# A windowed-attention and gated-product layer on one core: first chunk, load order, norms, transposes and last sums rearranged

## The chip, the core and the metric

The kernel runs on one core of a Trainium2 chip. The metric is the device time of one execution in microseconds (us), less is better. Three runs of the kernel before took 300.75 to 302.93 us, median 301.21.

## The reference, cut to what matters

```python
# x: 1 x 2048 x 512, wqkv: 512 x 1536, wo: 512 x 512, w_gate and w_up: 512 x 1792, w_down: 1792 x 512, all bf16
xn = (x - mean(x)) / sqrt(var(x) + 1e-5)              # over the 512 columns of a token
q, k, v = split_heads(xn @ wqkv)                      # 32 heads of 16
scores = q @ k.T * 16 ** -0.5                         # each token sees itself and the 255 before it
o = softmax(where(0 <= i - j < 256, scores, -1e9)) @ v
a = merge_heads(o) @ wo
b = ((xn @ w_gate) * (xn @ w_up)) @ w_down
out = x + a + b
```

## The kernel before

The 2048 tokens are 4 chunks (T = 0 to 3) of 4 blocks (b) of 128 tokens. Everything but the attention is a dense product of a chunk or a block. Attention goes by head group c (4 of 8 heads each), parity par (even or odd heads) and strip i (three strips of key blocks, `GROUPS`): 4 x 4 x 2 x 3 = 96 steps.

A step of `scores` runs four rows of the PE array side by side into S, one tile of four PSUM banks of which there is only one (`ps_s`); ScalarE takes exp of it into a P buffer (`ppool`, 5 buffers), and GpSimd zeroes what the window leaves out, with one `affine_select` for each masked block. Two steps later (LAG = 2), when all three strips of a head set are there, `values` multiplies them with V into `accb`; V has a column of ones, so that row 16 is the sum of the softmax. VectorE transposes `accb` (at), takes the reciprocal (rz), scales (on) and transposes again (OT).

The dense work is a list of fillers (`fillers`), each with a cost in units: one unit is a TensorE product of 512 columns. The order of the list is, for each T: down products and finish of the chunk before, 14 gate and up pairs of this chunk (`gu`), then V, K and Q of the next (`project`). Between the pairs of chunk T stand the norms of chunk T + 1: statistics, scale, apply and a transpose through TensorE of cost 1 (`norms`). `run` issues after each step so many fillers that the list is used up in proportion to the weight of the steps done, less a RESERVE of 28 units that is left over at the last step; a filler may have a step before which it must come and a `values` after which it may come. Of what is left, up to 22 units come ahead of the last `values`, the rest behind it, and at last the four `finish_late`.

TensorE, ScalarE, VectorE and GpSimd each run their instructions in the order in which they are written. The `ps_m` pool has 3 PSUM banks (tag M) for all dense sums: gp, up, psd, qkp, vp, xTp and last. `work` has 3 buffers of each tag, y among them.

The start (`setup`, then the loop in `run`): the four first blocks of x are loaded on the SP queue, Wqkv in three pieces (V columns, K, Q) on the ACT queue, then x 4 to 7, Wg and Wu by halves, x 8 to 15, Wd and Wo on SP. 36 products with an identity keep TensorE busy meanwhile (L85). Then each block b of chunk 0 is normalised (L114 to L133), transposed (L145, copied out by ScalarE at L148), multiplied for K and Q of head group 0 (`proj_qk_block`, L183) and for V (`proj_v`, L157), one block after the other. In later chunks VectorE copies the transposes out (L150).

The end: `finish_early` (L298 to L303) multiplies a block of the last chunk by three of the four parts of Wo, and VectorE adds x and keeps the sum in SBUF (y0); `finish_late` multiplies the last part into a fresh bank (last), VectorE adds y0 and the block is stored on SP.

Of the kernel before, what the change touches and what calls it, by code (L numbers as in the profile page):

```python
# [22 lines left out]
class Kernel:  # L23
    def __init__(self, ctx, tc, x, wqkv, wo, wg, wu, wd, out):
        self.tc, self.nc = tc, tc.nc
        _, S, D = x.shape
        self.S, self.D, self.F = S, D, wg.shape[1]
        assert D == 512 and S % 512 == 0 and self.F % 256 == 0
        self.NT, self.NCH, self.NF = S // 128, S // 512, self.F // 128
        self.x_d, self.out_d = x.flatten_outer_dims(), out.flatten_outer_dims()  # L30
        self.w_d = dict(qkv=wqkv, o=wo, g=wg, u=wu, d=wd)

        def pool(name, bufs, **kw):
            return ctx.enter_context(tc.tile_pool(name=name, bufs=bufs, **kw))

        self.const = pool("const", 1)
        self.chunk2 = pool("chunk2", 2)
        self.chunk3 = pool("chunk3", 3)
        self.ppool = pool("ppool", 5)
        self.work = pool("work", 3)  # L40
        self.xpool = pool("xpool", 4)
        self.small = pool("small", 4)
        self.ps_s = pool("ps_s", 1, space=bass.MemoryType.PSUM)
        self.ps_a = pool("ps_a", 1, space=bass.MemoryType.PSUM)
        self.ps_m = pool("ps_m", 3, space=bass.MemoryType.PSUM)


    def setup(self):
# [35 lines left out]
        for _ in range(36):  # L84
            nc.tensor.matmul(wps[:], lhsT=ident[:], rhs=ident[:], start=True, stop=True)  # L85
# [51 lines left out]
    def norm_transpose(self, t, on_act=False):  # L137
        nc = self.nc
        xn = self.xns.pop(t)
        T, b = divmod(t, 4)  # L140
        if b == 0:
            self.xnT[T] = self.chunk2.tile([128, 4, 512], BF16, tag="xnT", name=f"xnT{T}")
# [3 lines left out]
        dst = self.xnT[T][:, :, 128 * b:128 * b + 128]  # L146
        if on_act:
            nc.scalar.activation(out=dst, in_=ps[:], func=ACT.Copy)  # L148
        else:
            nc.vector.tensor_copy(out=dst, in_=ps[:])  # L150

    def proj_v(self, t):
        nc = self.nc
        T, b = divmod(t, 4)
        ps = self.ps_m.tile([128, 512], F32, tag="M", name="vp")
        for k in range(4):
            nc.tensor.matmul(ps[:], lhsT=self.xnT[T][:, k, 128 * b:128 * b + 128],  # L157
                             rhs=self.Wqkv[:, k, 1024:1536], start=(k == 0), stop=(k == 3))
# [3 lines left out]
    def proj_qk(self, T, c, is_k):  # L162
        nc = self.nc
        lo = 512 * is_k + 128 * c
        ps = self.ps_m.tile([128, 512], F32, tag="M", name="qkp")
        for k in range(4):
            nc.tensor.matmul(ps[:], lhsT=self.Wqkv[:, k, lo:lo + 128], rhs=self.xnT[T][:, k, :],  # L167
                             start=(k == 0), stop=(k == 3))
        if is_k:
            nc.vector.tensor_copy(out=self.K[T][:, c, :], in_=ps[:])  # L170
            nc.vector.tensor_scalar(out=self.Ko[T][:, c, :], in0=self.K[T][:, c, :],
                                    scalar1=self.odd[:, 0:1], scalar2=None, op0=ALU.mult)
        else:
            nc.vector.tensor_copy(out=self.Q[T][:, c, :], in_=ps[:])

    def proj_qk_block(self, b):

        nc = self.nc
        tok = slice(128 * b, 128 * b + 128)
        ps = self.ps_m.tile([128, 2, 128], F32, tag="M", name="qkb")  # L180
        for j, lo in enumerate((512, 0)):
            for k in range(4):
                nc.tensor.matmul(ps[:, j, :], lhsT=self.Wqkv[:, k, lo:lo + 128],  # L183
                                 rhs=self.xnT[0][:, k, tok], start=(k == 0), stop=(k == 3))
        nc.vector.tensor_copy(out=self.K[0][:, 0, tok], in_=ps[:, 0, :])
        nc.vector.tensor_copy(out=self.Q[0][:, 0, tok], in_=ps[:, 1, :])
# [68 lines left out]
    def gate(self, T, f):  # L255
        nc = self.nc
        if f == 0:
            self.hT[T] = self.const.tile([128, self.NF, 512], BF16, tag="hT", name=f"hT{T}")
        ps = self.ps_m.tile([128, 512], F32, tag="M", name="gp")
        for k in range(4):  # L260
            nc.tensor.matmul(ps[:], lhsT=self.Wg[:, k, 128 * f:128 * f + 128], rhs=self.xnT[T][:, k, :],  # L261
                             start=(k == 0), stop=(k == 3))
        self.gsb = self.work.tile([128, 512], BF16, tag="gsb", name="gsb")
        nc.vector.tensor_copy(out=self.gsb[:], in_=ps[:])  # L264

    def up(self, T, f):
        nc = self.nc
        ps = self.ps_m.tile([128, 512], F32, tag="M", name="up")
        for k in range(4):
            nc.tensor.matmul(ps[:], lhsT=self.Wu[:, k, 128 * f:128 * f + 128], rhs=self.xnT[T][:, k, :],  # L270
# [3 lines left out]
    def down(self, T, b, lo, hi):  # L274
        nc = self.nc
        if lo == 0:
            self.psd = self.ps_m.tile([128, 512], F32, tag="M", name="psd")
        for f in range(lo, hi):
            nc.tensor.matmul(self.psd[:], lhsT=self.hT[T][:, f, 128 * b:128 * b + 128],  # L279
                             rhs=self.Wd[:, f, :], start=(f == 0), stop=False)  # L280

    def wo(self, T, b, cs, ps, first):
        for c in cs:
            self.nc.tensor.matmul(ps[:], lhsT=self.OT[T][:, c, 128 * b:128 * b + 128],  # L284
                                  rhs=self.Wo[:, c, :], start=first and c == cs[0], stop=(c == cs[-1]))

    def store(self, T, b, ps, rest):
# [3 lines left out]
        nc.vector.tensor_tensor(out=y[:], in0=ps[:], in1=rest, op=ALU.add)  # L291
        nc.sync.dma_start(out=self.out_d[128 * t:128 * t + 128, :], in_=y[:])

    def finish(self, T, b):
        self.wo(T, b, (0, 1, 2, 3), self.psd, False)
        self.store(T, b, self.psd, self.x[:, 4 * T + b, :])

    def finish_early(self, T, b):  # L298

        nc = self.nc  # L300
        self.wo(T, b, (0, 1, 2), self.psd, False)
        self.y0[b] = self.const.tile([128, 512], F32, name=f"y0{b}")
        nc.vector.tensor_tensor(out=self.y0[b][:], in0=self.psd[:], in1=self.x[:, 4 * T + b, :], op=ALU.add)  # L303

    def finish_late(self, T, b):
        ps = self.ps_m.tile([128, 512], F32, tag="M", name="last")
        self.wo(T, b, (3,), ps, True)
        self.store(T, b, ps, self.y0[b][:])


    def fillers(self):
# [26 lines left out]
        def norms(T):  # L338
            t = 4 * T
            at = {f: [] for f in range(NF)}  # L340
            for b in range(4):
                at[b].append((0, lambda b=b: self.norm_stats(t + b)))
                at[6 + b].append((0, lambda b=b: self.norm_apply(t + b)))
                at[8 + b].append((1, lambda b=b: self.norm_transpose(t + b)))
            at[4].append((0, lambda: self.norm_scale(t)))
            return at
# [5 lines left out]
        for c in range(1, 4):  # L352
            qk(0, c, 6 * c)
        for T in range(NCH):
            if T:
                down(T - 1, 0)
                for b in range(4):
                    if b:
                        down(T - 1, b)
                    add(4, lambda T=T, b=b: self.finish(T - 1, b), None, NG * T - 1)  # L360
            gu(T, norms(T + 1) if T + 1 < NCH else {})
# [10 lines left out]
    def run(self):  # L372
        self.xns, self.stats, self.y0 = {}, {}, {}
        self.setup()
        NCH, NG, LAG = self.NCH, 24, 2
        RESERVE = 28
        self.new_chunk(0)
        self.norm_stats(0, 1)
        self.norm_scale(0, 1)
        for b in range(4):  # L380
            if b < 3:
                self.norm_stats(b + 1, 1)
                self.norm_scale(b + 1, 1)
            self.norm_apply(b)
            self.norm_transpose(b, True)
            self.proj_qk_block(b)
            self.proj_v(b)
        nc = self.nc
        nc.vector.tensor_scalar(out=self.Ko[0][:, 0, :], in0=self.K[0][:, 0, :],
                                scalar1=self.odd[:, 0:1], scalar2=None, op0=ALU.mult)  # L390
# [32 lines left out]
        fill(spent + 22, -1)  # L423
# [42 lines left out]
```

## Time and profile before

| | |
|---|---|
| runs of before | 300.75, 301.21, 302.93 us (median 301.21) |
| the profiled execution | 300.87 us, its span 299.1 us |
| TensorE matmuls busy | 274.7 us, 92% of the span |
| VectorE, ScalarE, GpSimd busy | 194.3, 181.5, 156.8 us |
| HBM read, written | 9.70 MB, 2.10 MB |

The span runs from the first to the last instruction of the execution; what lies around it is 1.8 us here. PE is TensorE, PEld its weight loads, DVE VectorE, ACT ScalarE, POOL GpSimd, SPq and ACTq the queues on which loads and stores are issued; "xTp<-ident,xn" reads "writes xTp from ident and xn", and L145 is line 145 of the kernel. Ends of matmuls are modelled, so a group of products is best read from one start to the next start.

### The profile page before, as it was taken

What the parts mean: (1) busy time and instruction counts of PE and PEld (TensorE: products, weight loads), DVE (VectorE), ACT (ScalarE), POOL (GpSimd) and SP (SyncE); (2) the same over time, 40 slices, a digit from 0 to 9 for tenths busy, and PEclk for the clock granted to TensorE, in tenths of its full rate; (3) what the DMA queues carried; (4) which work ended last, traced back from release to release, by engine and by line L of the source; (5) the groups of instructions that cost most, each with busy time, mean ns of one, the idle gap of its engine ahead of it and who ended that gap; (6) DMA issues with size and microseconds to landing.
All of it is one profiled execution on the core that took longest, in us unless ns stands there. A gap on an engine that the chain in (4) does not pass through costs nothing.

```text
span 299.1 us, 5877 instructions
## 1 busy us (share of the span) xinstructions
PE 274.7 (92%) x2424; PEld 119.6 (40%) x2460; DVE 194.3 (65%) x362; ACT 181.5 (61%) x118; POOL 156.8 (52%) x266
## 2 busy tenths in 40 slices
PE   6569989999999999999999999999999999999992
PEld 5333333433433444444344444443444443344440
DVE  3238898985823599984942489985763357877325
ACT  1247566568766756669566666758766675756610
POOL 3115565455565556656555466655556555555620
PEclk9999999999999999999999999999999999999998
DMA  7999000000000100000000000000000000000001
GB/s 234 370 369 324 3 3 0 3 0 2 1 20 18 37 0 2 1 2 2 0 19 19 20 18 3 0 2 1 2 0 20 35 20 1 2 0 2 2 0 70
DMA packets 10506, 12.17 MB, mean 41 GB/s; under 512 B 496, under 2 KB 10480, under 8 KB 10480
## 3 DMA queue, kind: packets, MB, share of 16 engines
q1 hardware_dynamic: 8896, 10.23, 10.1%
q10 hardware_dynamic: 1584, 1.57, 1.7%
q8 instruction: 19, 0.31, 0.4%
q14 instruction: 7, 0.06, 0.1%
HBM read 9.70 MB, written 2.10 MB: 39 GB/s over the span
## 4 chain that ended last, share of the span: by engine, by line
PE 68%; ACT 17%; DVE 6%; DMA 3%; issue 3%; POOL 1%; ACTq 1%; DVEq 0%
ACT P L209 16%; PE psd L279 15%; PE up L270 12%; PE gp L261 11%; PE S L201 10%; PE accb L234 7%; PE qkp L167 6%; DMA Wqkv<-in_A_wqkv_dram 3%; PE vp L157 2%; PE psd L284 2%; DVE at L245 1%; PE xTp L145 1%; DVE hT L272 1%; DVE st L114 1%; PE qkb L183 1%
## 5 line engine op out<-in xcount | busy, mean ns | idle before, releaser
L209 ACT ACTIVATE P<-S 128x2048 bf16<-128x2048 f32 (+2 forms) x96 | 170.0, 1771 | 86.8 <-PE S L201 79.1
L214 POOL TENSOR_SCALAR_AFFINE_SELECT P<-P 128x512 bf16<-128x512 bf16 x128 | 81.8, 639 | 75.2 <-ACT P L209 74.6
L218 POOL TENSOR_SCALAR_AFFINE_SELECT P<-P 128x512 bf16<-128x512 bf16 x112 | 72.8, 650 | 42.4 <-ACT P L209 42.4
L261 PE MATMUL gp<-xnT,Wg 128*128 128x512 bf16 x213 | 57.1, 380 | 1.4 <-DVE gsb L264 0.5
L270 PE MATMUL up<-xnT,Wu 128*128 128x512 bf16 x216 | 57.3, 380 | 0.5
L279 PE MATMUL psd<-Wd,hT 128*128 128x512 bf16 x213 | 51.7, 380 | 1.4 <-issue 1.3
L272 DVE TENSOR_TENSOR hT<-up,gsb 128x512 bf16<-128x512 f32 x56 | 38.5, 687 | 11.0 <-PE up L270 8.0
L245 DVE STREAM_TRANSPOSE at<-accb 128x512 f32<-128x512 f32 x32 | 22.9, 715 | 32.6 <-PE accb L234 32.2
L264 DVE CAST gsb<-gp 128x512 bf16<-128x512 f32 x56 | 38.1, 680 | 3.7 <-PE gp L261 3.4
L270 PEld LDWEIGHTS <-Wu 128*128 128x128 bf16 x224 | 19.9, 98 | 25.8 <-issue 5.4
L279 PEld LDWEIGHTS <-hT 128*128 128x128 bf16 x224 | 19.8, 97 | 25.9 <-issue 5.3
L261 PEld LDWEIGHTS <-Wg 128*128 128x128 bf16 x224 | 19.8, 98 | 25.0 <-issue 6.0
L167 PE MATMUL qkp<-xnT,Wqkv 128*128 128x512 bf16 x117 | 27.5, 380 | 0.5 <-issue 0.5
L234 PE MATMUL accb<-P,V 128*17 128x384 bf16 (+2 forms) x704 | 25.4, 276 | 0.0
L291 DVE TENSOR_TENSOR y<-psd,x 128x512 bf16<-128x512 f32 x12 | 8.3, 692 | 23.2 <-PE psd L284 23.2
L201 PE MATMUL S<-Q,Ko 32*128 32x256 bf16 (+2 forms) x352 | 18.4, 275 | 3.8 <-ACT P L209 3.6
L201 PE MATMUL S<-Q,K 16*128 16x256 bf16 (+2 forms) x352 | 18.4, 275 | 2.6 <-ACT P L209 2.4
L234 PEld LDWEIGHTS <-V 128*17 128x17 bf16 x704 | 13.8, 90 | 8.7 <-issue 5.5
L167 PEld LDWEIGHTS <-Wqkv 128*128 128x128 bf16 x120 | 10.7, 98 | 13.7 <-issue 2.5
L157 PE MATMUL vp<-Wqkv,xnT 128*128 128x512 bf16 x61 | 15.9, 392 | 0.3 <-issue 0.2
L201 PEld LDWEIGHTS <-Ko 32*128 32x128 bf16 x352 | 6.9, 92 | 22.6 <-issue 22.1
L201 PEld LDWEIGHTS <-K 16*128 16x128 bf16 x352 | 6.6, 92 | 22.6 <-issue 22.5
(44 smaller groups left out, 172.2 us busy)
## 6 DMA issues: line engine op xcount, KB each, us to landing
out_dram<-y SPq DMA_DIRECT2D x16, 128.0 KB, 1.7
Wg<-in_B_w_gate_dram SPq DMA_DIRECT2D x2, 896.0 KB, 9.9
Wu<-in_B_w_up_dram SPq DMA_DIRECT2D x2, 896.0 KB, 11.5
Wd<-in_B_w_down_dram SPq DMA_DIRECT2D x1, 1792.0 KB, 17.7
Wqkv<-in_A_wqkv_dram ACTq DMA_DIRECT2D x3, 512.0 KB, 6.0
x<-in_A_x_dram SPq DMA_DIRECT2D x1, 1024.0 KB, 14.6
x<-in_A_x_dram SPq DMA_DIRECT2D x4, 128.0 KB, 5.1
x<-in_A_x_dram SPq DMA_DIRECT2D x1, 512.0 KB, 8.2
```

The source lines that it names most:

```text
L167: nc.tensor.matmul(ps[:], lhsT=self.Wqkv[:, k, lo:lo + 128], rhs=self.xnT[T][:, k, :], start=(k == 0), stop=(k == 3))
L201: nc.tensor.matmul(S[:, e, col:col + n], lhsT=(self.Ko if par else self.K)[U][rows, c, 128 * j:128 * j + 128], rhs=self.Q[T][rows, c, 128 ...
L209: nc.scalar.activation(out=P[:, :, lo:hi], in_=S[:, :, lo:hi], func=ACT.Exp, scale=0.25)
L214: nc.gpsimd.affine_select(out=P[:, :, j:j + 128], in_=P[:, :, j:j + 128], pattern=[[0, 4], [1, 128]], compare_op=ALU.is_ge, fill=0.0, base ...
L218: nc.gpsimd.affine_select(out=P[:, :, j:j + 128], in_=P[:, :, j:j + 128], pattern=[[0, 4], [-1, 128]], compare_op=ALU.is_gt, fill=0.0, bas ...
L234: nc.tensor.matmul(acc[32 * e:32 * e + 17, 128 * q0:128 * q0 + n], lhsT=self.V[U][:, v, 8 * c + 2 * e + par, 0:17], rhs=P[:, e, col:col + ...
L245: nc.vector.transpose(out=at.rearrange("p b r -> p (b r)"), in_=acc[:])
L261: nc.tensor.matmul(ps[:], lhsT=self.Wg[:, k, 128 * f:128 * f + 128], rhs=self.xnT[T][:, k, :], start=(k == 0), stop=(k == 3))
L264: nc.vector.tensor_copy(out=self.gsb[:], in_=ps[:])
L270: nc.tensor.matmul(ps[:], lhsT=self.Wu[:, k, 128 * f:128 * f + 128], rhs=self.xnT[T][:, k, :], start=(k == 0), stop=(k == 3))
L272: nc.vector.tensor_tensor(out=self.hT[T][:, f, :], in0=ps[:], in1=self.gsb[:], op=ALU.mult)
L279: nc.tensor.matmul(self.psd[:], lhsT=self.hT[T][:, f, 128 * b:128 * b + 128], rhs=self.Wd[:, f, :], start=(f == 0), stop=False)
```

## The change

Five things are changed.

- Loads: everything goes on the SP queue in one order: x block 0, x block 1, x blocks 2 and 3, Wqkv's V, K and Q columns, the first halves of Wg and Wu, x 4 to 7, the second halves, Wd, Wo, x 8 to 15.
- First chunk (`first_chunk`): the norms run a block ahead of the transposes, the transposes a block ahead of V; K and Q of head group 0 are made for the whole chunk at once behind the four blocks, and K of head group 1 too. ScalarE copies Q out. There are 42 warm-up products in place of 36.
- Norms of later chunks: those of chunk 1 stand beside the gate and up products of chunk 0, with one block for every three pairs; those of chunks 2 and 3 stand beside the down products of the chunk before theirs. Each block has its own scale. The transpose is a DMA from the SP queue, of cost 0; `xnT` is laid out by block, then by part of the 512 columns.
- Last sums: the sums of the last chunk stay in PSUM, blocks 0 and 1 in banks of `ps_m`, blocks 2 and 3 in the four banks that S used. x is added to blocks 0 and 2 by a product with the identity, and to blocks 1 and 3 by VectorE on the way out; ScalarE copies blocks 0 and 2 out and stores them on the ACT queue.
- Sizes: 6 P buffers for 5, RESERVE 38 for 28, and up to 24 units for 22 ahead of the last `values`.

```diff
@@ pools and loads @@
-        self.ppool = pool("ppool", 5)
+        self.ppool = pool("ppool", 6)
...
-        for t in range(4):
-            nc.sync.dma_start(out=self.x[:, t, :], in_=xv[:, t, :])
+        for lo, hi in ((0, 1), (1, 2), (2, 4)):
+            nc.sync.dma_start(out=self.x[:, lo:hi, :], in_=xv[:, lo:hi, :])
         for lo in (1024, 512, 0):
-            nc.scalar.dma_start(out=self.Wqkv[:, :, lo:lo + 512], in_=wq[:, :, lo:lo + 512])
+            nc.sync.dma_start(out=self.Wqkv[:, :, lo:lo + 512], in_=wq[:, :, lo:lo + 512])
         h = self.F // 2
-        nc.sync.dma_start(out=self.x[:, 4:8, :], in_=xv[:, 4:8, :])
         for lo in (0, h):
             nc.sync.dma_start(out=self.Wg[:, :, lo:lo + h], in_=wg[:, :, lo:lo + h])
             nc.sync.dma_start(out=self.Wu[:, :, lo:lo + h], in_=wu[:, :, lo:lo + h])
-        nc.sync.dma_start(out=self.x[:, 8:NT, :], in_=xv[:, 8:NT, :])
+            if lo == 0:
+                nc.sync.dma_start(out=self.x[:, 4:8, :], in_=xv[:, 4:8, :])
...
+        nc.sync.dma_start(out=self.x[:, 8:NT, :], in_=xv[:, 8:NT, :])
...
-        for _ in range(36):
+        for _ in range(42):
@@ transposes @@
+            self.xnT[T] = self.chunk2.tile([128, 4, 4, 128], BF16, tag="xnT", name=f"xnT{T}")
+        if by_dma:
+            nc.sync.dma_start_transpose(out=self.xnT[T][:, b, :, :], in_=xn[:])
+            return
...
+        nc.scalar.activation(out=self.xnT[T][:, b, :, :], in_=ps[:], func=ACT.Copy)
...
-            nc.tensor.matmul(ps[:], lhsT=self.Wqkv[:, k, lo:lo + 128], rhs=self.xnT[T][:, k, :],
+            nc.tensor.matmul(ps[:], lhsT=self.Wqkv[:, k, lo:lo + 128], rhs=self.xnT[T][:, :, k, :],
@@ the first chunk (proj_qk_block and the loop in run go) @@
+    def first_chunk(self):
+        self.new_chunk(0)
+        for b in range(2):
+            self.norm_stats(b, 1)
+            self.norm_scale(b, 1)
+        for b in range(4):
+            self.norm_apply(b)
+            if b < 2:
+                self.norm_stats(b + 2, 1)
+                self.norm_scale(b + 2, 1)
+        self.norm_transpose(0, False)
+        for b in range(4):
+            if b < 3:
+                self.norm_transpose(b + 1, False)
+            self.proj_v(b)
+        self.proj_qk(0, 0, 1)
+        self.proj_qk(0, 0, 0, True)
+        self.proj_qk(0, 1, 1)
@@ down, store, finish @@
+            if T == self.NCH - 1 and b >= 2:
+                if b == 2:
+                    self.four = self.ps_s.tile([128, 4, 512], F32, tag="S", name="four")
+                self.psd = self.four[:, b, :]
+            else:
+                self.psd = self.ps_m.tile([128, 512], F32, tag="M", name="psd")[:]
...
+        if add:
+            nc.vector.tensor_tensor(out=y[:], in0=ps, in1=self.x[:, t, :], op=ALU.add)
+        else:
+            nc.scalar.activation(out=y[:], in_=ps, func=ACT.Copy)
+        (nc.sync if add else nc.scalar).dma_start(out=self.out_d[128 * t:128 * t + 128, :], in_=y[:])
...
     def finish_early(self, T, b):
-        self.wo(T, b, (0, 1, 2), self.psd, False)
-        self.y0[b] = self.const.tile([128, 512], F32, name=f"y0{b}")
-        nc.vector.tensor_tensor(out=self.y0[b][:], in0=self.psd[:], in1=self.x[:, 4 * T + b, :], op=ALU.add)
+        self.wo(T, b, (0, 1, 2), self.psd)
+        if b % 2 == 0:
+            self.nc.tensor.matmul(self.psd, lhsT=self.ident[:], rhs=self.x[:, 4 * T + b, :],
+                                  start=False, stop=False)
+        self.sums[b] = self.psd
 
     def finish_late(self, T, b):
-        ps = self.ps_m.tile([128, 512], F32, tag="M", name="last")
-        self.wo(T, b, (3,), ps, True)
-        self.store(T, b, ps, self.y0[b][:])
+        self.wo(T, b, (3,), self.sums[b])
+        self.store(T, b, self.sums[b], b % 2 == 1)
@@ fillers and run @@
+        def norms(T, at, step):
+            t, out = 4 * T, {}
             for b in range(4):
+                for k, f in enumerate((lambda b=b: self.norm_stats(t + b, 1),
+                                       lambda b=b: self.norm_scale(t + b, 1),
+                                       lambda b=b: self.norm_apply(t + b),
+                                       lambda b=b: self.norm_transpose(t + b, True))):
+                    out.setdefault(at + step * b + (0, 0, 1, 1)[k], []).append((0, f))
+            return out
...
-        for c in range(1, 4):
+        add(4, lambda: self.proj_qk(0, 1, 0), 6)
+        for c in range(2, 4):
             qk(0, c, 6 * c)
         for T in range(NCH):
             if T:
+                todo = norms(T + 1, 0, 1) if T + 1 < NCH else {}
                 for b in range(4):
+                    for g in todo.get(b, ()):
+                        add(*g)
+                    down(T - 1, b)
                     add(4, lambda T=T, b=b: self.finish(T - 1, b), None, NG * T - 1)
-            gu(T, norms(T + 1) if T + 1 < NCH else {})
+            for g in todo.get(4, ()) if T else ():
+                add(*g)
+            gu(T, norms(1, 1, 3) if T == 0 else {})
...
-        RESERVE = 28
+        RESERVE = 38
+        self.first_chunk()
...
-        fill(spent + 22, -1)
+        fill(spent + 24, -1)
```

## Rows read from the trace of the kernel before

**Rows 1.** Windows of 10 us: each engine's busy us (instructions), granted clock, DMA share, GB/s.
```profile
0.00:10.00 10.00, 5.21 (x44) 4.52 (x44) 2.88 (x9) 2.08 (x3) 2.79 (x13) 1.00 0.86 264
10.00:20.00 10.00, 6.43 (x43) 3.35 (x45) 3.95 (x13) 3.47 (x6) 1.71 (x4) 1.00 1.06 379
...
230.00:240.00 10.00, 9.84 (x91) 4.04 (x91) 3.52 (x7) 5.85 (x4) 6.00 (x10) 1.00 0.08 28
```

**Rows 2.** Waits of PE: us in total, times, longest us.
```profile
PE S L201 <- ACT P L209: 6.1, 23, 0.6
...
PE last L284 <- DVE OT L251: 0.7, 1, 0.7
PE gp L261 <- DVE gsb L264: 0.5, 1, 0.5
...
PE xTp L145 <- DVE xnT L150: 0.2, 1, 0.2
```

**Rows 3.** Timeline of the start: start us, us, engine, line, out<-in, count [idle before <-releaser].
```profile
1.42 4.02 PE L85 MATMUL wps<-ident 128*128 128x128 bf16 x36 [1.42 <-POOL ident L78]
...
3.31 0.69 DVE L114 BATCH_NORM_STATS2 st<-x 128x6 f32<-128x512 bf16 x1 [1.48 <-DMA x<-in_A_x_dram]
...
4.04 0.18 DVE L115 BATCH_NORM_AGGREGATE mv<-st 128x2 f32<-128x6 f32 x1
...
4.62 0.58 POOL L125 TENSOR_TENSOR rs<-ve,mhalf 128x1 f32<-128x1 f32 x1
...
6.40 0.38 DVE L133 TENSOR_SCALAR xn<-x,mv,rs 128x512 bf16<-128x512 bf16 x1
...
7.48 0.60 ACT L148 ACTIVATE xnT<-xTp 128x512 bf16<-128x512 bf16 x1 [3.57 <-PE xTp L145]
...
10.37 0.61 PE L183 MATMUL qkb<-xnT,Wqkv 128*128 128x128 bf16 x4 [1.65 <-DMA Wqkv<-in_A_wqkv_dram]
...
12.68 0.61 PE L145 MATMUL xTp<-ident,xn 128*128 128x128 bf16 x4
...
13.97 0.61 PE L183 MATMUL qkb<-xnT,Wqkv 128*128 128x128 bf16 x8 [0.69 <-ACT xnT L148]
...
14.41 1.03 PE L157 MATMUL vp<-Wqkv,xnT 128*128 128x512 bf16 x4
...
21.40 0.34 PE L201 MATMUL S<-Q,K 16*128 16x384 bf16 x4
...
28.23 1.04 PE L261 MATMUL gp<-xnT,Wg 128*128 128x512 bf16 x4
```

**Rows 4.** The chain that ended last: start us, us, what, matmuls.
```profile
66.86 0.61 PE vp L157 x2
...
109.93 0.86 PE up L270 x4
```

**Rows 5.** Timeline of TensorE beside chunk 1's gate and up products.
```profile
127.97 0.39 PE L145 MATMUL xTp<-ident,xn 128*128 128x128 bf16 x4
128.21 1.02 PE L261 MATMUL gp<-xnT,Wg 128*128 128x512 bf16 x4
```

**Rows 6.** Timeline of the end.
```profile
283.33 1.88 ACT L209 ACTIVATE P<-S 128x2048 bf16<-128x2048 f32 x1 [1.27 <-PE S L201]
...
289.71 0.83 PE L234 MATMUL accb<-P,V 128*17 128x128 bf16 x24
...
292.87 0.95 PE L284 MATMUL last<-Wo,OT 128*128 128x512 bf16 x3 [0.70 <-DVE OT L251]
293.31 1.87 DVE L291 TENSOR_TENSOR y<-last,y 128x512 bf16<-128x512 f32 x3
...
295.83 0.69 DVE L291 TENSOR_TENSOR y<-last,y 128x512 bf16<-128x512 f32 x1 [0.66 <-DMA out_dram<-y]
```

**Rows 7.** DMA issues: out<-in, queue, count, KB each, median us to landing.
```profile
out_dram<-y SPq DMA_DIRECT2D x16, 128.0 KB, 1.7
...
x<-in_A_x_dram SPq DMA_DIRECT2D x1, 1024.0 KB, 14.6
```

More of the change, by code (lines that the diff above doesn't have):

```diff
@@ L135, in norm_apply, with norm_transpose @@
         self.xns[t] = xn
-    def norm_transpose(self, t, on_act=False):
+    def norm_transpose(self, t, by_dma):
         nc = self.nc
@@ L141, in norm_transpose @@
         if b == 0:
-            self.xnT[T] = self.chunk2.tile([128, 4, 512], BF16, tag="xnT", name=f"xnT{T}")
+            self.xnT[T] = self.chunk2.tile([128, 4, 4, 128], BF16, tag="xnT", name=f"xnT{T}")
+        if by_dma:
+            nc.sync.dma_start_transpose(out=self.xnT[T][:, b, :, :], in_=xn[:])
+            return
         ps = self.ps_m.tile([128, 4, 128], BF16, tag="M", name="xTp")
@@ L145, in norm_transpose @@
             nc.tensor.transpose(ps[:, k, :], xn[:, 128 * k:128 * k + 128], self.ident[:])
[L146 to L150, printed above, removed]
+        nc.scalar.activation(out=self.xnT[T][:, b, :, :], in_=ps[:], func=ACT.Copy)
     def proj_v(self, t):
@@ L156, in proj_v @@
         for k in range(4):
-            nc.tensor.matmul(ps[:], lhsT=self.xnT[T][:, k, 128 * b:128 * b + 128],
+            nc.tensor.matmul(ps[:], lhsT=self.xnT[T][:, b, k, :],
                              rhs=self.Wqkv[:, k, 1024:1536], start=(k == 0), stop=(k == 3))
@@ L160, in proj_v, with proj_qk @@
                              func=ACT.Copy)
-    def proj_qk(self, T, c, is_k):
+    def proj_qk(self, T, c, is_k, on_act=False):
         nc = self.nc
@@ L172, in proj_qk @@
                                     scalar1=self.odd[:, 0:1], scalar2=None, op0=ALU.mult)
+        elif on_act:
+            nc.scalar.activation(out=self.Q[T][:, c, :], in_=ps[:], func=ACT.Copy)
         else:
             nc.vector.tensor_copy(out=self.Q[T][:, c, :], in_=ps[:])
[L176 to L186, printed above, removed]
+    def first_chunk(self):
[16 more added lines that the diff above has]
+        self.proj_qk(0, 1, 1)
     def parts(self, T, i):
@@ L260, in gate @@
         for k in range(4):
-            nc.tensor.matmul(ps[:], lhsT=self.Wg[:, k, 128 * f:128 * f + 128], rhs=self.xnT[T][:, k, :],
+            nc.tensor.matmul(ps[:], lhsT=self.Wg[:, k, 128 * f:128 * f + 128], rhs=self.xnT[T][:, :, k, :],
                              start=(k == 0), stop=(k == 3))
@@ L269, in up @@
         for k in range(4):
-            nc.tensor.matmul(ps[:], lhsT=self.Wu[:, k, 128 * f:128 * f + 128], rhs=self.xnT[T][:, k, :],
+            nc.tensor.matmul(ps[:], lhsT=self.Wu[:, k, 128 * f:128 * f + 128], rhs=self.xnT[T][:, :, k, :],
                              start=(k == 0), stop=(k == 3))
@@ L276, in down, with wo, store @@
         if lo == 0:
-            self.psd = self.ps_m.tile([128, 512], F32, tag="M", name="psd")
+            if T == self.NCH - 1 and b >= 2:
[4 more added lines that the diff above has]
+                self.psd = self.ps_m.tile([128, 512], F32, tag="M", name="psd")[:]
         for f in range(lo, hi):
-            nc.tensor.matmul(self.psd[:], lhsT=self.hT[T][:, f, 128 * b:128 * b + 128],
+            nc.tensor.matmul(self.psd, lhsT=self.hT[T][:, f, 128 * b:128 * b + 128],
                              rhs=self.Wd[:, f, :], start=(f == 0), stop=False)
-    def wo(self, T, b, cs, ps, first):
+    def wo(self, T, b, cs, ps):
         for c in cs:
-            self.nc.tensor.matmul(ps[:], lhsT=self.OT[T][:, c, 128 * b:128 * b + 128],
-                                  rhs=self.Wo[:, c, :], start=first and c == cs[0], stop=(c == cs[-1]))
-    def store(self, T, b, ps, rest):
+            self.nc.tensor.matmul(ps, lhsT=self.OT[T][:, c, 128 * b:128 * b + 128],
+                                  rhs=self.Wo[:, c, :], start=False, stop=(c == 3))
+    def store(self, T, b, ps, add):
         nc = self.nc
@@ L290, in store @@
         y = self.work.tile([128, 512], BF16, tag="y", name="y")
-        nc.vector.tensor_tensor(out=y[:], in0=ps[:], in1=rest, op=ALU.add)
-        nc.sync.dma_start(out=self.out_d[128 * t:128 * t + 128, :], in_=y[:])
+        if add:
[3 more added lines that the diff above has]
+        (nc.sync if add else nc.scalar).dma_start(out=self.out_d[128 * t:128 * t + 128, :], in_=y[:])
     def finish(self, T, b):
-        self.wo(T, b, (0, 1, 2, 3), self.psd, False)
-        self.store(T, b, self.psd, self.x[:, 4 * T + b, :])
+        self.wo(T, b, (0, 1, 2, 3), self.psd)
+        self.store(T, b, self.psd, True)
     def finish_early(self, T, b):
-        nc = self.nc
-        self.wo(T, b, (0, 1, 2), self.psd, False)
-        self.y0[b] = self.const.tile([128, 512], F32, name=f"y0{b}")
-        nc.vector.tensor_tensor(out=self.y0[b][:], in0=self.psd[:], in1=self.x[:, 4 * T + b, :], op=ALU.add)
+        self.wo(T, b, (0, 1, 2), self.psd)
[3 more added lines that the diff above has]
+        self.sums[b] = self.psd
     def finish_late(self, T, b):
-        ps = self.ps_m.tile([128, 512], F32, tag="M", name="last")
-        self.wo(T, b, (3,), ps, True)
-        self.store(T, b, ps, self.y0[b][:])
+        self.wo(T, b, (3,), self.sums[b])
+        self.store(T, b, self.sums[b], b % 2 == 1)
     def fillers(self):
@@ L336, in gu @@
                     add(*g)
-        def norms(T):
-            t = 4 * T
-            at = {f: [] for f in range(NF)}
+        def norms(T, at, step):
+            t, out = 4 * T, {}
             for b in range(4):
[L342 to L346, printed above, removed]
+                for k, f in enumerate((lambda b=b: self.norm_stats(t + b, 1),
[4 more added lines that the diff above has]
+            return out
         def down(T, b):
@@ L355, in fillers @@
             if T:
-                down(T - 1, 0)
+                todo = norms(T + 1, 0, 1) if T + 1 < NCH else {}
                 for b in range(4):
-                    if b:
-                        down(T - 1, b)
+                    for g in todo.get(b, ()):
+                        add(*g)
+                    down(T - 1, b)
                     add(4, lambda T=T, b=b: self.finish(T - 1, b), None, NG * T - 1)
-            gu(T, norms(T + 1) if T + 1 < NCH else {})
+            for g in todo.get(4, ()) if T else ():
+                add(*g)
+            gu(T, norms(1, 1, 3) if T == 0 else {})
             if T + 1 < NCH:
@@ L372, in run @@
     def run(self):
-        self.xns, self.stats, self.y0 = {}, {}, {}
+        self.xns, self.stats, self.sums = {}, {}, {}
         self.setup()
         NCH, NG, LAG = self.NCH, 24, 2
-        RESERVE = 28
[L377 to L390, printed above, removed]
+        RESERVE = 38
+        self.first_chunk()
         steps = [(T, c, par, i) for T in range(NCH) for c in range(4) for par in range(2) for i in range(3)]
```

## The prediction

> **What bounds the kernel now.** I read the windows first. In a window of the middle TensorE is busy 9.84 of 10 us, while VectorE, ScalarE and GpSimd have 3.5 to 6.0 us of work; in the first two windows TensorE is busy 5.21 and 6.43 us [rows 1]. So the middle is bound by TensorE's own work, and the start by something else. The waits of TensorE say how little can be won in the middle: it waits 6.1 us for the softmax engine in 23 short pieces, and under 1 us for anything else [rows 2]. The timeline of the start shows what holds it: the warm-up products end at 5.44, block 0's `xn` is made at 6.40, a K/Q product then waits until 10.37 for Wqkv, and the first scores begin at 21.40 [rows 3]. At the end the last values product starts at 289.71, TensorE waits 0.70 us for OT, and the fourth y waits 0.66 us for a store, because there are three y buffers [rows 6]. So 21.4 us lie before the first scores, 8.5 us behind the last values product, and about 269 us between, nearly all of it matmuls. A group of four 512-column products takes 0.86 us in the chain [rows 4], 0.216 us each; I call that one unit.
>
> **Start.** The loads' order changes, not their sum. 2.64 MB have moved by 10 us (264 GB/s over 10 us), and 379 GB/s is the rate of the next window [rows 1]. In the new order the V columns of Wqkv end at 1.05 MB, K at 1.57, Q at 2.10. If no stretch is faster than 379 GB/s, these pass by 10 - 1.59/0.379 = 5.8 us, 7.2 and 8.6 us; Wg's first half (3.0 MB) and Wu's (3.9 MB) by 11 and 13.4 us, x 4 to 7 by 14.8 us. None of these is late: V is needed at about 7.4 us, K at 12, the first gate product today at 28.23 [rows 3], so about 22 then. The wait until 10.37 goes.
>
> What is late next is the chain of norms. Block 0's statistics start about 3.2 us (3.31 today, with Wqkv sharing the engines); from there to the end of `rs` is 1.89 us (3.31 to 4.62 + 0.58), so `xn` 0 is ready at about 5.6. Each further block costs VectorE 0.69 + 0.18 + 0.38 = 1.25 us [rows 3]: 6.85, 8.1, 9.2. The warm-ups are 36 in 4.02 us, 0.112 us each, so 42 of them end at about 6.1 us: they, not the norm, release block 0's transposes. Those take 0.61 us (as at 12.68) and their copy 0.60 [rows 3]: `xnT` 0 stands at 7.35, while block 1 is transposed. V of block 0 then takes between 1.03 us (the row at 14.41) and twice that: a warm-up of 128 columns takes 0.112 us where a quarter of a unit is 0.054, a ratio of two, so the start runs at the lower of TensorE's two levels (1.2 GHz, though the granted clock reads 1.00), and the transposes at 12.68 still take the long time [rows 3]. I take 1.5: 8.9. Behind it come two blocks' transposes (0.25 to 0.4 each), and six groups of 0.86 us (three V, then K, Q and the K of group 1): 8.9 + 0.7 + 5.2 + 0.2 = 15.0 us to the first scores. ScalarE's eight copies (four xnT, four V at 0.60) and Q's fit beside this: Q's group ends about 14.2 and its copy at 14.9, under the K of group 1. Bounds: 14.3 if V 0 is already fast, 17.0 if the level rises no earlier than today (about 13 us), when three groups cost 0.86 more each. Gain at the start 21.4 - 15.0 = **6.4 us** (4.4 to 7.1).
>
> The K group of head group 1 is done there and leaves the paced work: **0.9 us** more.
>
> **Transposes of chunks 1 to 3.** Twelve TensorE transposes go. From one transpose's start to the next product is 0.24 us [rows 5], 0.25 with the switches: 12 x 0.25 = **3.0 us**. With them go twelve VectorE copies, and two waits of the first chunk, 0.2 for `xnT` and 0.5 for a `gsb` behind it [rows 2]: **0.7 us**. The norms of chunks 2 and 3 move beside the down products, where VectorE has 3.5 us of work in 10 [rows 1]. GpSimd gets twelve `rs` of 0.58 us (and their adds) instead of three larger ones, where it is busy 6.0 of 10 us; masks may come later by one of these, and the sixth P buffer and the two steps of lag cover that.
>
> The DMA transposes are in no row. Nearest rows: a 128 KB store lands in 1.7 us, a 1 MB load among other loads in 14.6 us [rows 7]; I take 5 us for a block, nearer the store in size. What hides it: in the first chunk the blocks are issued three gate/up pairs apart. Gate 0 starts at 28.23 and the next chunk's V at 66.86 [rows 3, 4], 2.76 us a pair, so 8.3 us apart, and the last block has two pairs and three V products, about 8.9 us. In later chunks the last transpose is a whole gate/up stage (28 groups, 24 us) ahead. Cost 0. On the SP queue the stores stand behind transposes that wait for `xn`; VectorE makes that promptly in this stage. A page of the Trainium skill speaks against this part: "VectorE: DVE Perf Modes", The three transpose paths, has a 128x128 transpose at 390 ns on TensorE and 1309 ns through the DMA, and its rules prefer TensorE where a PSUM destination will do. By it a block takes an estimated 4 x 1.3 = 5.2 us, which changes nothing in the sum as long as the time is hidden. No run here shows it yet.
>
> `xnT` is now laid out by block, so gate, up, K and Q products (28 x 4 x 4 + 8 x 4 x 4 = 576) read their moving operand in four runs of 128 columns. No row shows such a read. Below, nothing; above, I take four separate 128-column products: the eight at 13.97 take 0.61 us, 0.17 of it latency (1.03 less 0.86 for a group), so (0.61 - 0.17)/8 x 4 = 0.22 us a unit [rows 3], up to 6 ns over 0.216, so 3.4 us. I take 0, since the columns stay in one instruction.
>
> **Pacing.** The work list falls from 912 to 896 units and the reserve rises from 28 to 38, so a full step gets 9.5 units, not 9.8. More steps hold only two groups of four: 2 x 0.86 + 0.4 is less than an exp of 1.88 us and its start, and then the next scores wait for S, 0.27 us a time [rows 2]. About four more such waits: **+0.9 us**.
>
> **End.** Behind the last scores twelve units (2.6 us) are left before the third block's sums need S's banks, and the exp that must release them takes 1.88 us [rows 6]: no wait. Behind the last values product 12 units stand instead of 7, 2.6 us against a VectorE chain of 2.3 us (290.54 to 292.87), so the 0.70 us wait goes [rows 6]. Two identity products add 2 x 0.216 us. From the first late product to the end stays 6.2 us: ScalarE's copies spread the work, but the fourth y still needs the first one's buffer, so its store must land first, as at 295.83. Sum **-0.3 us**.
>
> **Sum.** -6.4 - 0.9 - 3.0 - 0.7 + 0.9 - 0.3 = -10.4 us. The profiled run took 300.87 us with a span of 299.1, within 0.1% of the median of 301.21; from the median this gives **290.8 us**.
>
> **Rivals.**
> A. The low level lasts: the first scores come at 17.0. Speaks for it: the transposes at 12.68 are slow today. Against: TensorE now works from 1.42 to 15 almost without a pause. 292.8 and up to 294.
> B. The other side: DMA transposes are slow and queue on SP. With D us a block, the fourth block of the first chunk lands 4D after the first's issue; it is needed 3 x 8.3 + 8.9 = 33.8 us after. From D = 8.5 TensorE waits 4D - 33.8 at the chunk's V. Past D = 11.8 us the wait is 13.4 us: slower than before by over 1% (304); at 11 the gain is gone (301). Later chunks have some 50 us for their four. For it: 14.6 us for 1 MB under load; against: 1.7 us for the same 128 KB.
> C. The four-run reads cost: 6 ns each give 294.2; 13 ns would take it within 1%.
> D. TensorE's freed time goes to the exp loop: each step without a values product (two thirds of some 80) waits 0.27 us, 14 us at most less today's 6.1, 4 to 7 us beyond my 0.9: 295 to 298.
>
> **Chances.** The forecast 0.64 (own range 288.5 to 293), A 0.10, C 0.09, D 0.07, B 0.10 (half of it within 1%, half slower). Within 1% (298.2 to 304.2) is about what no change looks like in this measurement. Faster 0.88 (forecast, A, most of C and D), same 0.07, slower 0.05. Range 287 to 296.5: below by the early start, no waits and a ppool that frees the exp (together 3.5 us); above it takes in A, C and the half of D.
>
> **What would show it.** The first scores near 15 us, with no wait for Wqkv; xnT transposes landing in about 5 us and no wait of V products on them; gate products still 0.86 us a group; S waits of TensorE near 7 us; no OT wait at the end, but still one wait for a store before the last y. A first-scores time above 17, a group above 0.88 us, or V products waiting for a DMA would each break a step.

## The result

The changed kernel takes 290.75 us (median of 4 runs, 290.48 to 292.21) against 301.39 for the kernel before (4 runs): ratio 0.965, 95% interval 0.960 to 0.970. The forecast was 290.8. Its profiled execution has a span of 289.2 us, 9.9 less than before's 299.1. (That execution took 292.21 us, 3.0 more than its span where the others have 1.7 to 1.8, so I go by spans inside a trace.) Some later runs of the kernel before have a lower mean granted clock (0.965 to 0.973) and take 302.5 to 305.2 us, so small differences are better read from spans than from a ratio.

The timeline of its start (columns as in [rows 3]):

```profile
1.42 4.66 PE L86 MATMUL wps<-ident 128*128 128x128 bf16 x42 [1.42 <-POOL ident L79]
...
5.88 1.27 PE L150 MATMUL xTp<-ident,xn 128*128 128x128 bf16 x8
...
7.20 1.07 PE L158 MATMUL vp<-Wqkv,xnT 128*128 128x512 bf16 x4
...
11.41 2.75 PE L168 MATMUL qkp<-xnT,Wqkv 128*128 128x512 bf16 x12
...
14.09 0.34 PE L212 MATMUL S<-Q,K 16*128 16x384 bf16 x4
```

The first scores start at 14.09, not 21.40, which is 7.3 us earlier, and no wait of TensorE for Wqkv is left. The waits of TensorE in the whole span (to set against [rows 2]):

```profile
PE S L212 <- ACT P L220: 7.7, 31, 0.7
PE four L300 <- ACT y L311: 1.5, 1, 1.5
...
PE up L281 <- DVE gsb L275: 0.5, 2, 0.3
```

The waits for S grew from 6.1 to 7.7 us, and a new wait of 1.5 us stands at the end. Beside the dense products TensorE waited 1.0 us for VectorE in the kernel before: 0.5 for gsb (VectorE's copy of a gate product) and 0.2 for xnT [rows 2], and 0.3 for hT (the gated product):

```profile
PE gp L261 <- DVE hT L272: 0.3, 1, 0.3
```

Now it waits 0.5 us, all of it for gsb. The end (columns as in [rows 6]):

```profile
279.52 0.83 PE L245 MATMUL accb<-P,V 128*17 128x128 bf16 x24
...
283.31 0.60 ACT L311 ACTIVATE y<-psd 128x512 bf16<-128x512 f32 x1 [9.36 <-PE psd L300]
...
285.17 0.38 PE L300 MATMUL four<-Wo,OT 128*128 128x512 bf16 x1 [1.47 <-ACT y L311]
285.82 0.69 DVE L309 TENSOR_TENSOR y<-four,x 128x512 bf16<-128x512 f32 x1 [1.61 <-DMA out_dram<-y]
```

And the DMA issues (as [rows 7], without a size): a transposed block lands 2.4 us after its issue (median of twelve).

```profile
xnT<-xn SPq DMA_TRANSPOSE x12, 2.4
```

From the first scores to the last values product the kernel before takes 289.71 - 21.40 = 268.3 us, the changed one 279.52 - 14.09 = 265.4: 2.9 us less. Behind the start of the last values product it takes 9.7 us where before took 9.4, but with 12 units there for 7 (1.1 us) and so 0.8 us less for the rest.

### The profile page after: what moved, and what is told of

Same layout as the page of the kernel before. It is cut to its first block, busy times and chain, and to the rows that moved or that the text cites. A ratio compares the mean times of both kernels' runs of the same rounds, so it can differ in the third digit from the quotient of the medians.

```text
span 289.2 us, 5817 instructions
## 1 busy us (share of the span) xinstructions
PE 274.1 (95%) x2396; PEld 116.8 (40%) x2396; DVE 185.1 (64%) x337; ACT 183.3 (63%) x121; POOL 161.7 (56%) x284
## 4 chain that ended last, share of the span: by engine, by line
PE 67%; ACT 22%; DVE 6%; issue 2%; POOL 1%; DMA 1%; ACTq 0%; DVEq 0%; POOLq 0%
ACT P L220 21%; PE psd L295 15%; PE S L212 10%; PE gp L272 9%; PE up L281 9%; PE accb L245 7%; PE qkp L168 5%; PE psd L300 3%; PE vp L158 3%; PE four L295 2%; PE wps L86 2%; DVE gsb L275 1%; DVE hT L283 1%; DVE at L256 1%; POOL P L225 1%
## 5 line engine op out<-in xcount | busy, mean ns | idle before, releaser
L272 PE MATMUL gp<-xnT,Wg 128*128 128x512 bf16 x224 | 57.8, 380 | 0.0
L295 PE MATMUL psd<-Wd,hT 128*128 128x512 bf16 x196 | 47.1, 380 | 0.0
L295 PEld LDWEIGHTS <-hT 128*128 128x128 bf16 x224 | 20.2, 98 | 25.9 <-issue 4.5
L168 PE MATMUL qkp<-xnT,Wqkv 128*128 128x512 bf16 x128 | 30.6, 380 | 0.0
L309 DVE TENSOR_TENSOR y<-psd,x 128x512 bf16<-128x512 f32 x13 | 9.0, 689 | 21.4 <-PE psd L300 21.4
L168 PEld LDWEIGHTS <-Wqkv 128*128 128x128 bf16 x128 | 11.3, 98 | 14.6 <-issue 2.9
L212 PEld LDWEIGHTS <-K 16*128 16x128 bf16 x352 | 7.4, 92 | 23.8 <-issue 23.3
L171 DVE CAST K<-qkp 128x512 bf16<-128x512 f32 x16 | 11.0, 687 | 8.5 <-PE qkp L168 8.4
```

The costliest lines, as they stand in the source:

```text
L212: nc.tensor.matmul(S[:, e, col:col + n], lhsT=(self.Ko if par else self.K)[U][rows, c, 128 * j:128 * j + 128], rhs=self.Q[T][rows, c, 128 ...
L295: nc.tensor.matmul(self.psd, lhsT=self.hT[T][:, f, 128 * b:128 * b + 128], rhs=self.Wd[:, f, :], start=(f == 0), stop=False)
```

## The experiments

**The start in two halves.** Three kernels put the new load order, the new first chunk with its 42 warm-ups, or both into the kernel before.

```diff
 loads:  the setup part of the change, nothing else
 chunk:  the kernel before with
+        self.first_chunk()                                # as in the change, xnT laid out as before
+        for _ in range(42):
...
+        add(4, lambda: self.proj_qk(0, 1, 0), 6)          # K of head group 1 leaves the list
 start:  loads and chunk
```

> The kernel before with the new load order alone. Theory that the start is bound by its chain of norms, copies and products: only the wait of the first K/Q product for Wqkv shortens, the first scores come about 2 us earlier (19.5), ratio 0.993. Rival, that the loads bind the start: first scores at 16 or before, ratio 0.98.

> The kernel before with the new first chunk and 42 warm-ups, loads as before (Wqkv on the ACT queue, beside x). Theory that the chain binds: first scores about 15.5 us, ratio 0.977. Rival, that the loads bind: the blocks of x and Wqkv arrive as late as before, first scores at 18 or later, ratio above 0.985.

> The kernel before with the new load order, the new first chunk and 42 warm-ups, all else as before. Theory that the parts add up: the first scores come at 14.1 us as in the changed kernel and the K group of head group 1 leaves the paced work, so the time falls by 7.3 + 0.9 = 8.2 us, ratio 0.973. Rival, that the earlier start is given back in waits for S or for weights in the first chunk: scores at 14.1, but the time falls by less than 5 us.

| kernel | first scores | span | median | ratio (95%) |
|---|---|---|---|---|
| before | 21.40 | 299.1 | 302.48 | |
| loads | 22.00 | 299.5 | 301.99 | 0.999 (0.994 to 1.004) |
| chunk | 17.54 | 296.3 | 298.51 | 0.986 (0.979 to 0.993) |
| start | 14.06 | 292.9 | 294.51 | 0.973 (0.964 to 0.981) |

(The median of before is that of 13 runs on the chip of these three kernels, 300.77 to 305.22 us; the ratios are to it. First scores and spans are those of the profiled executions.) The halves do not add up. With the load order alone the first scores come 0.6 us later, against both expectations; with the first chunk alone they come 3.9 us earlier, between the two expectations; with both, 7.3 us earlier. The timeline of TensorE in `loads` shows why the first is lost:

```profile
5.32 0.61 PE L146 MATMUL xTp<-ident,xn 128*128 128x128 bf16 x4
9.12 0.40 PE L184 MATMUL qkb<-xnT,Wqkv 128*128 128x128 bf16 x4 [3.19 <-DMA Wqkv<-in_A_wqkv_dram]
10.55 0.61 PE L184 MATMUL qkb<-xnT,Wqkv 128*128 128x128 bf16 x4 [1.03 <-DMA Wqkv<-in_A_wqkv_dram]
10.95 1.91 PE L158 MATMUL vp<-Wqkv,xnT 128*128 128x512 bf16 x4
```

Block 0's transposes start 1.5 us earlier (at 5.32; 6.84 in the kernel before), but the old first chunk wants K and Q first, which are now behind x and V in one queue. TensorE stands still from 6 to 9.1 us, and the two V products that follow take 1.91 and 1.83 us, not 1.03. Here the windows show the clock itself (granted clock before the DMA share):

```profile
6.00:8.00 2.00, 0.00 (x0) 0.00 (x0) 0.00 (x0) 0.56 (x1) 0.00 (x0) 1.00 0.98 310
8.00:10.00 2.00, 0.40 (x4) 0.23 (x4) 0.00 (x0) 0.00 (x0) 0.00 (x0) 0.94 1.07 357
10.00:12.00 2.00, 1.45 (x7) 0.86 (x8) 0.81 (x3) 0.00 (x0) 0.00 (x0) 0.50 1.05 397
```

After the idle stretch the granted clock is 0.50, the lower level (1.2 GHz). In `chunk` the late blocks of x do the same: TensorE waits 1.28 and 1.78 us for `xn`, and the clock of the windows from 8 to 12 us is 0.62 and 0.53:

```profile
6.94 0.40 PE L145 MATMUL xTp<-ident,xn 128*128 128x128 bf16 x4 [1.28 <-DVE xn L133]
9.12 0.61 PE L145 MATMUL xTp<-ident,xn 128*128 128x128 bf16 x4 [1.78 <-DVE xn L133]
9.52 1.91 PE L157 MATMUL vp<-Wqkv,xnT 128*128 128x512 bf16 x4
```

```profile
8.00:10.00 2.00, 0.88 (x6) 0.61 (x7) 1.93 (x6) 0.24 (x1) 0.89 (x3) 0.62 1.11 350
10.00:12.00 2.00, 2.00 (x10) 0.99 (x9) 0.65 (x2) 0.89 (x3) 0.89 (x2) 0.53 1.07 378
```

So x must come first and the products must ask for V first; either alone leaves TensorE waiting, and in these two traces the wait is paid a second time in the clock. A page of the Trainium skill says the same of the cause: "TensorE: Matmul & The Clock Gate", HAM oscillation, has the clock fall after a stretch in which TensorE idles; these windows agree (0.94, then 0.50). Not every wait is paid twice: in a trace below (`p5`) TensorE waits 0.58 us at the same place and stays fast.

`start` also answers its rival in part. It gains 7.3 us at the first scores and 0.9 for the K group, but the span falls by 6.2 only: its waits for S rise from 6.1 to 7.8 us, 1.7 us given back. So neither the theory (8.2 us) nor the rival (less than 5) came. The totals do not decide it: `start` is 8.0 us below the median of before on its chip and 6.9 below the 301.39 us of the result, and the ratio's interval is too wide to tell 6 from 8.

**The warm-ups (`w36`).**

```diff
-        for _ in range(42):
+        for _ in range(36):
```

> The changed kernel with 36 warm-up products for 42. Theory that the warm-ups only delay block 0: its transposes start at about 5.4 us for 5.88, the norms of blocks 1 to 3 then bind, and the first scores come 0 to 0.5 us earlier. Rival, that six more warm-ups bring TensorE to its upper level sooner: the first V product takes 1.9 us for 1.07 and the first scores come 1 to 3 us later.

290.47 us (290.43 to 290.81), first scores at 13.65, 0.44 earlier. Block 0's transposes start at 5.36 and are slow (0.61 us), those of block 1 take 0.40 and V 1.03. So, set against this execution, the six more warm-ups bought nothing and cost the 0.4 us that they take; in the total that is too small to tell from the changed kernel's 290.75. But the rival is not dead: the kernel `best` below also has 36, and in its profiled execution block 1's transposes are still slow:

```profile
6.43 0.61 PE L151 MATMUL xTp<-ident,xn 128*128 128x128 bf16 x4 [0.51 <-DVE xn L135]
```

Its first V product then takes 1.86 us, and the first scores come at 15.87, as the rival has it. In every trace here that has the new loads, the new first chunk and 42 warm-ups, the first V product takes 1.02 to 1.07 us. Whether six more warm-ups guard the start is open.

**TensorE transposes at the new places (`pet` and `pet2`).** In the changed kernel the later chunks' transposes go through TensorE again (four products of cost 1, VectorE copies them out); once right behind each norm, as the DMA is in the list, and once two places further on.

```diff
-            nc.sync.dma_start_transpose(out=self.xnT[T][:, b, :, :], in_=xn[:])
-            return
+            ...   # four nc.tensor.transpose into xTp, then
+            nc.vector.tensor_copy(out=self.xnT[T][:, b, :, :], in_=ps[:])
...
-                    out.setdefault(at + step * b + (0, 0, 1, 1)[k], []).append((0, f))
+                    out.setdefault(at + step * b + (0, 0, 1, 1)[k], []).append((int(k == 3), f))   # pet
+                    out.setdefault(at + step * b + (0, 0, 1, 3)[k], []).append((int(k == 3), f))   # pet2
...
-            for g in todo.get(4, ()) if T else ():             # pet2, and chunk 1's norms one place earlier
-                add(*g)
-            gu(T, norms(1, 1, 3) if T == 0 else {})
+            gu(T, norms(1, 0, 3) if T == 0 else {f - 4: todo[f] for f in todo if f >= 4})
```

> The changed kernel with the later chunks' transposes on TensorE, copied out by VectorE as in the kernel before, at their new places and with cost 1 in the list. Theory that a TensorE transpose costs its own time: twelve of 0.25 us, 3.0 us slower than the changed kernel, some 293.7 us. Rival, that the freed time goes to the waits for S: 1 us slower or less.

> The changed kernel with the later chunks' transposes on TensorE, two places of the list (two gate and up pairs, or two blocks of down products) behind their norms. Theory that a transpose on TensorE costs its own time where the norm is done by then, and that the 22 us of the run with transposes right behind their norms are waits of TensorE for xn: 3 us slower than the changed kernel, some 293.7 us. Rival, that a TensorE transpose costs more than its time at the new places (PSUM banks, copies): 8 us slower or more.

`pet` takes 312.19 us (310.50 to 314.90), ratio 1.035 (1.025 to 1.045): slower than the kernel before. Neither expectation held. The waits of TensorE say why, and the timeline what the longest of them brings:

```profile
PE xTp L147 <- DVE xn L134: 17.2, 13, 2.5
PE S L212 <- ACT P L220: 5.9, 24, 0.7
```

```profile
29.42 0.45 PE L147 MATMUL xTp<-ident,xn 128*128 128x128 bf16 x4 [2.50 <-DVE xn L134]
29.66 1.91 PE L272 MATMUL gp<-xnT,Wg 128*128 128x512 bf16 x4
```

Thirteen waits for `xn`, up to 2.5 us, twelve of them at the later chunks' transposes: TensorE runs in order, and a transpose written right behind its norm waits for VectorE, GpSimd's `rs` and VectorE again. On SP only stores stand behind the same wait. Behind the longest wait a gate group takes 1.91 us, not 1.03, and the granted clock of the window from 31 to 33 us is 0.50. 17.2 and twelve times 0.25 make 20.2 of the 21.4 us; the waits for S are 1.8 us fewer than in the changed kernel, and slow stretches such as this one weigh against that.

`pet2`, with the norm two places ahead as in the kernel before, takes 294.06 (293.57 to 295.77): 3.3 us more than the changed kernel, where 3.0 was expected, and no long wait for `xn`. The agreement is partly chance. Its waits of TensorE differ from the changed kernel's in two lines above all:

```profile
PE S L212 <- ACT P L220: 6.1, 25, 0.7
PE gp L272 <- DVE gsb L275: 2.1, 1, 2.1
```

Twelve transposes of 0.25 us are 3.0; the wait for gsb and one of 0.3 for xnT, for 0.5 in the changed kernel, add 1.9; the waits for S are 1.6 us fewer. So, by these rows, about half of the 3.0 us that the DMA transposes free comes back as waits for S, and the waits for VectorE that fall away bring the gain back to 3 us. Besides, the DMA lets norm and transpose be written at one place.

**Doubled DMA transposes (`dup`).**

```diff
...   # scratch: a tile of its own for each chunk
+            nc.sync.dma_start_transpose(out=self.scratch[:, b, :, :], in_=xn[:])
             nc.sync.dma_start_transpose(out=self.xnT[T][:, b, :, :], in_=xn[:])
```

> The changed kernel with every DMA transpose issued twice, first into a scratch tile. Theory that the DMA transposes lie wholly beside other work: within 0.5 us of the changed kernel although SP and the DMA engines carry twice the transposes. Rival, that they hold something up (the V products, or stores and y buffers behind them on SP): 1.5 us slower or more.

290.81 us (290.71 to 290.95): twice the transposes cost nothing that can be measured. They are hidden.

**The place of the norms, the P buffers, the end (`place`, `p5`, `oldtail`).** Three parts of the changed kernel undone one at a time.

```diff
 place:
-                todo = norms(T + 1, 0, 1) if T + 1 < NCH else {}
+                todo = {}
-            gu(T, norms(1, 1, 3) if T == 0 else {})
+            gu(T, norms(T + 1, 1, 3) if T + 1 < NCH else {})
 p5:
-        self.ppool = pool("ppool", 6)
+        self.ppool = pool("ppool", 5)
 oldtail:
-        RESERVE = 38
+        RESERVE = 28
...   # fill(spent + 22); finish_early and finish_late with y0 and a fresh bank, as before
```

> The changed kernel with the norms of chunks 2 and 3 beside the gate and up products (one block for every three pairs, as for chunk 1) in place of beside the down products; transposes by DMA. Theory that VectorE's load beside the gate and up products does not bind TensorE: within 0.5 us of the changed kernel. Rival, that the new place is what pays: 2 us slower or more, with TensorE waiting for gsb and hT.

> The changed kernel with 5 P buffers for 6. Theory that TensorE binds and the sixth buffer only frees ScalarE (its waits for GpSimd return from 2.8 to about 8 us): 0 to 0.7 us slower. Rival, that the sixth buffer pays: 2 us slower or more.

> The changed kernel with the end of the kernel before: sums of the last chunk added to x by VectorE and kept in SBUF, a last product into a fresh bank, a reserve of 28 units and 22 of them ahead of the last values product. Theory: the end brings next to nothing, 0 to 0.7 us slower, because the wait for OT (0.7 us) returns and two identity products (0.43 us) go. Rival, that keeping the sums in PSUM pays: 2 us slower.

`place` takes 292.20 us (291.81 to 292.79), 1.45 more: between the two expectations. TensorE then waits 1.7 us for `gsb` beside the gate and up products, where the changed kernel waits 0.5; that is 1.2 of it. Both kernels have a scale for each block, so this compares two places for the new norms; in the kernel before, with one scale for four blocks beside the gate and up products, the wait for gsb was 0.5 us.

```profile
PE up L281 <- DVE gsb L275: 1.7, 3, 1.1
```

`p5` takes 291.13 (290.95 to 291.81), `oldtail` 290.91 (290.54 to 291.06): 0.4 and 0.2 us, no difference that these runs can tell. In `p5` ScalarE waits 4.5 us for the masks, in the changed kernel 2.8, and TensorE's waits for S are 7.7 us in both. The start of `p5` holds the wait named above, and V behind it is fast:

```profile
7.33 1.02 PE L158 MATMUL vp<-Wqkv,xnT 128*128 128x512 bf16 x4 [0.58 <-DMA Wqkv<-in_A_wqkv_dram]
```

`oldtail` puts the reserve back as well, and its waits for S are 0.8 us fewer than in the changed kernel, so what the new end brings by itself is not shown:

```profile
PE S L212 <- ACT P L220: 6.9, 26, 0.7
```

**The end (`ybuf` and `best`).** Two waits of the same length stand there: the late product of block 3 writes into the tile `four` and waits for ScalarE to read block 2 from it, and block 3's y waits for the first store, for want of a fourth y buffer.

```diff
 ybuf and best:
-        y = self.work.tile([128, 512], BF16, tag="y", name="y")
+        y = self.ypool.tile([128, 512], BF16, tag="y", name="y")     # pool of 4
 best also: 36 warm-ups, and
+        for b in range(4):
+            self.wo(T, b, (3,), self.sums[b])
+        for b in range(4):
+            self.store(T, b, self.sums[b], b % 2 == 1)
```

> The changed kernel with four y buffers of their own in place of three. Theory of the two equal waits: the wait for the first store goes, the wait of the late product for ScalarE's copy stays, so 0 to 0.3 us. Rival, that the y buffer alone holds the end: 1.3 us or more faster.

> The changed kernel with 36 warm-ups, the four late products of the last chunk all ahead of the four copies, and four y buffers of their own. Theory that the end is held by two waits of the same length, the late product of block 3 for ScalarE's copy of block 2 (1.5 us) and block 3's y for the first store (1.6 us): with both gone and 0.4 us from the warm-ups some 1.8 us faster than the changed kernel, 289 us. Rival, that the store of the last y lands no earlier: within 0.5 us.

`ybuf` takes 290.57 us (290.07 to 291.49), 0.2 less than the changed kernel: the wait for the store gives way to the one for the late product, as the theory has it. `best` takes 289.81 (289.57 to 291.95), ratio to before 0.959 (0.954 to 0.964), 0.9 less than the changed kernel where I expected 1.8. Its end shows the third in line, block 3's y behind ScalarE's copy of block 2:

```profile
281.29 0.83 PE L246 MATMUL accb<-P,V 128*17 128x128 bf16 x24
...
286.21 0.60 ACT L312 ACTIVATE y<-four 128x512 bf16<-128x512 f32 x1 [0.54 <-DVE y L310]
...
286.84 0.69 DVE L310 TENSOR_TENSOR y<-four,x 128x512 bf16<-128x512 f32 x1 [0.86 <-ACT y L312]
```

That copy in turn had waited 0.54 us for VectorE's y of block 1. From the last values product to the last y's start the changed kernel, `ybuf` and `best` take 6.30, 5.98 and 5.55 us: 0.75 won of 1.6. Why a read by VectorE follows a read by ScalarE in another bank of the tile I have not tried. `best` beats both kernels, by little over the changed one, and its start is not safe: in its profiled execution (span 290.2, its other runs 287.8 to 288.1) TensorE, not yet fast at block 1's transposes, waited 0.41 us for Wqkv's V, the first V product took 1.86 us, and the first scores came at 15.87.

```profile
7.46 1.86 PE L159 MATMUL vp<-Wqkv,xnT 128*128 128x512 bf16 x4 [0.41 <-DMA Wqkv<-in_A_wqkv_dram]
```

## Why the prediction was right

The mechanism held: the start pays most, the transposes leave TensorE and stay hidden on the DMA, and the middle stays bound by TensorE. But that the total is only 0.05 us off is luck, since errors of opposite sign cancelled. By spans the time fell by 9.9 us for the 10.4 of the sum: the start brought 0.9 more than forecast, everything behind the first scores 2.6 us where the sum has 4.0. Of the 1.4 missing there the waits for S are 0.7 and VectorE's waits 0.2; some 0.5 I have not placed.

- The start: 6.4 us forecast, 7.3 measured. The step that was off most is V of block 0, for which I took 1.5 us between the two levels; it took 1.07, nearly the 1.03 of the later groups. What stands behind it, two transposes and six groups, took 5.8 us (8.3 to 14.1) where I had summed 6.1.
- That nothing of the loads is late held, but not by the margin I gave. I let a piece land when its bytes had passed; in `loads` K was used at 9.12 and Q at 10.55 where I had 7.2 and 8.6, 1.9 us later. In the changed kernel's trace V, K and Q landed at 6.4, 7.9 and 9.4, 0.6 to 0.8 us later than I had, so the lateness differs between executions. There K and Q are wanted at 11.4 and later, but V at 7.2, and in two of the later traces (`best` and `p5`) TensorE waits 0.4 and 0.6 us for it.
- The transposes: 3.0 us forecast, 3.3 by `pet2`, where it is a sum of several waits. Cost 0 for the DMA transposes was right (`dup`); a block took 2.4 us for the 5 that I took, and the store of the same size (1.7) was the better neighbour. Rival B had its threshold at 8.5.
- VectorE's waits: 0.7 forecast, 0.5 measured, and not the same ones: the 0.2 for xnT went, and 0.3 for hT, but the 0.5 for gsb that I had counted stands as before. `place` shows that with a scale for each block the norms of chunks 2 and 3 are 1.45 us better off beside the down products, a choice that I priced at nothing.
- Pacing: +0.9 us forecast for four more waits for S; there are eight more, +1.6. The cause is open. The reserve may have a part (`oldtail`, with 28: 26 waits, 6.9 us), and so may the transposes that left the list (`pet2`, with a reserve of 38: 25 waits, 6.1 us); but `start`, with the old reserve and transposes on TensorE, has 28 waits and 7.8 us, and no run changes one of these alone in the kernel before. This is rival D at its foot, not at the 4 to 7 us that I gave it.
- The four-run reads cost nothing. The first gate group and the up group behind it start 0.87 us apart, as good as the 0.86 of [rows 4], and inside such groups the products start 216 ns apart in both traces (median), so rival C falls:

```profile
20.27 1.04 PE L272 MATMUL gp<-xnT,Wg 128*128 128x512 bf16 x4
21.14 1.03 PE L281 MATMUL up<-xnT,Wu 128*128 128x512 bf16 x4
```

- The end: 0.3 us forecast, `oldtail` 0.2 and not to be told from nothing, with the reserve in it. The wait for OT went, as written; the buffer wait stayed, as written; that the late product also waits for ScalarE I had not seen, and it cost nothing only because the store's wait is as long.
- Rival A did not come in the changed kernel, but it is real: in `loads`, `chunk` and one execution of `best` products at the lower level cost an estimated 1 to 2 us (V products of 1.8 to 1.9 us for 1.03).

## What to carry to other kernels

A load order and the order of the products that use the loads are one change: at the first scores either alone brought -0.6 and 3.9 us here, both 7.3, because each alone left TensorE waiting (3.19 us at once in `loads`, 1.28 and 1.78 in `chunk`) and the granted clock fell to about half behind it. A transpose by DMA was worth 3 us here where the norm stood well ahead, and where norm and transpose stand at one place far more, since an in-order engine would wait for the whole chain (17 us). TensorE time that is freed beside a second loop is not all won: by `pet2`'s rows about half of what the transposes freed came back as waits for S. At the end of a kernel look for the next wait before taking one away: here three stood behind each other, and two of them removed brought half of what they showed.

## What the runs showed of the hardware

A DMA transpose of a 128x512 bf16 block between two places in SBUF held the SP queue for 1.2 us and landed 2.4 us after its issue (medians of twelve; the slowest landed after 4.0). Issuing each of them twice changed the time by nothing that can be measured (`dup`). The page "VectorE: DVE Perf Modes" of the Trainium skill, The three transpose paths, has 1309 ns for a 128x128 transpose through the DMA, which would be an estimated 5.2 us for four in a row; the measured block takes less than half of that, so in this case the four parts of a block do not run one after the other at that price.
